# The second norm's factor moved behind the MLP's first product, the bias moved into gelu, one more bits buffer, four last transfers

## The chip, the core and the metric

The kernel runs on one core of a Trainium2 chip. The metric is the device time of one execution in microseconds (us). A core has five engines that run side by side: TensorE (PE in the profile; its weight loads are PEld), VectorE (DVE), ScalarE (ACT), GpSimd (POOL) and the sync engine (SP), which mostly issues DMA transfers. Three runs of the kernel before took 777.36 to 779.22 us, with a median of 778.76 us.

## What is computed

The input x has 2048 tokens of 512 values. It is normalised once (xn), and two branches read xn: attention with 32 heads of 16 values, and an MLP of width 1792 that normalises xn a second time. The result is x + attention(xn) + MLP(xn).

```python
xn = _layernorm(x)
q, k, v = split(xn @ wqkv)                 # 32 heads, Dh = 16
p = softmax(einsum("bhqd,bhkd->bhqk", q, k) * Dh ** -0.5)
attn = einsum("bhqk,bhkd->bqhd", p, v).reshape(B, S, D) @ wo
y = _layernorm(xn)
h = gelu(einsum("bsd,df->bsf", y, w1) + b1)  # tanh form, F = 1792
out = x + attn + einsum("bsf,fd->bsd", h, w2) + b2
```

As xn already has mean zero, the second norm is a product of each token's row with one number, 1 + r2[token].

## The kernel before, in words

Queries are cut into four tiles of 512 (qt) and heads into eight groups of four; a pair of these is a set g, 32 in all. For a set, keys come in 16 tiles of 128 (k). One unit is the score of one head against one key tile for 512 queries, a 128x512 block in PSUM (line 1037); there are 2048 units. Each unit takes one of two ways to its exponential. On the first, ScalarE reads two or three units at once (128x1024 or 128x1536) and writes exp to p_sb (line 1236). On the second, VectorE does it by bits for the four heads of a key tile together: four evictions write shifted 16-bit integers (128x512, line 1333, into ib, which lies in x_sb and in the tile it), and three more instructions of 128x2048 add constants to them (line 1354, TERMS = 4), so that the four bit patterns read as fp16 sum up to an approximation of exp. TensorE multiplies both kinds with the values va (line 1055) and sums them in one PSUM bank per set. NI is the number of bits buffers (five here; four of them are the space of x_sb), KD lists the seven key tiles of a set that may go by bits, and next_d decides when one is started; a key tile that is not started in time falls to ScalarE.

The MLP is done for each qt: build_mlp builds a 128x512 broadcast r2b of r2 (four products rt of r2 with ones on VectorE, line 1495, then TensorE, then a copy, line 1505), scales xnT into yT with two instructions of 128x2048 (lines 1507 and 1512), multiplies by w1 in 14 chunks (line 596 issues these), and adds b1 when VectorE evicts a chunk to ht (line 1528). After two query tiles, gelu runs in place over ht on ScalarE in one burst: four instructions of 128x3584 (line 1542) between two loads of activation tables. There are two such bursts. The product with w2 follows.

The order of all engines' instructions is set while the program is built, by a planner (_Plan): each piece has a cost, a due time (prio) and dependencies, and the planner places the piece that can start first on its engine, by due time among those that can start at nearly the same moment. KEEP favours a piece of the same TensorE mode as the one before. The planner's cost of a gelu burst is what tells it how long ScalarE is away; while it is, TensorE is given units for the bits way and matmuls with zeros (fill, line 1685) to do.

At the end, the last query tile's output is evicted by ScalarE and VectorE in turn into yT, and SP sends it in two transfers of 256 KB (build_final). At the start, the first norm's factor is made on GpSimd from the variance: an addition (line 743) and a power (line 745), for two token tiles at a time.

Of the kernel before, what the change touches and what calls it, by code (L numbers as in the profile page):

```python
# [1740 lines left out]
```

## Time and profile before

| what | value |
|---|---|
| median of three runs | 778.76 us (777.36 to 779.22) |
| profiled execution, its own time | 780.46 us |
| its span, first to last instruction | 778.7 us |
| mean granted TensorE clock | 0.991 of 2.4 GHz |
| ScalarE busy | 754.8 us, 97% |
| TensorE busy | 741.3 us, 95% |
| VectorE busy | 690.5 us, 89% |
| GpSimd busy | 49.4 us, 6% |

The profile is of one execution. Its own time is 1.7 us above the median of the runs, and its span is 1.8 us shorter than its own time. TensorE's busy time counts pipelined matmuls whose ends are modelled, and matmuls with zeros that fill gaps, so that its share is not a share of useful work. Busy time of ScalarE is the union of its instructions, which overlap at their ends.

### The profile page before, as it was taken

To read this page: it belongs to the slowest core of one execution; us is meant where nothing else is said; L and a number is where in the kernel's file an instruction comes from. 1 tells how busy PE (TensorE), PEld (TensorE's weight loads), DVE (VectorE), ACT (ScalarE), POOL (GpSimd) and SP (SyncE) were. 2 spreads that over 40 slices of the span, in tenths; PEclk is the share of its full clock that TensorE was granted. 3 is DMA by queue.
4 is the path that set the end of the run, shared out by engine and by line. 5 is a ranking of instruction groups with operands and counts; after the bars stand their busy time and mean duration, and the time that the engine had idled before them with its cause. 6 is when DMAs were issued, how large, how long until landed. Compare 5 with 4: busy or idle time off the path is not lost.

```text
span 778.7 us, 21921 instructions
## 1 busy us (share of the span) xinstructions
PE 741.3 (95%) x9344; PEld 242.0 (31%) x9344; DVE 690.5 (89%) x1196; ACT 754.8 (97%) x663; POOL 49.4 (6%) x81
## 2 busy tenths in 40 slices
PE   8999999999999999999899999999999989999996
PEld 3333223333323323333223333333233323333332
DVE  7857899999999988689999897989999999869795
ACT  5999899999999999999999999999999999999995
POOL 2300000020010000100001001100001000000001
PEclk9999899999999999999999999999999999999998
DMA  6300011234001300311010312320012101212001
GB/s 189 111 2 10 22 44 33 50 93 106 18 3 29 79 19 12 73 51 50 16 29 21 87 30 68 80 57 16 3 34 58 45 3 50 53 37 68 10 13 44
DMA packets 59157, 35.31 MB, mean 45 GB/s; under 512 B 41844, under 2 KB 50868, under 8 KB 59056
## 3 DMA queue, kind: packets, MB, share of 16 engines
q1 hardware_dynamic: 52576, 24.05, 11.3%
q0 software_dynamic: 4608, 8.39, 4.6%
q8 instruction: 74, 1.21, 0.7%
q10 hardware_dynamic: 1872, 1.44, 0.6%
q14 instruction: 27, 0.22, 0.1%
HBM read 26.08 MB, written 2.61 MB: 37 GB/s over the span
## 4 chain that ended last, share of the span: by engine, by line
ACT 37%; PE 32%; DVE 16%; issue 14%; DMA 0%; ACTq 0%; SPq 0%
ACT p_sb L1236 35%; PE ps L596 10%; PE ps L1037 10%; PE ps L1055 10%; DVE x_sb L1333 6%; DVE it L1354 4%; ACT ht L1542 1%; DVE it L1333 1%; DVE stats L731 1%; PE ps L1685 1%; DVE yT L1507 0%; DVE va L944 0%; DVE osb L1389 0%; DVE qc L918 0%; DMA x_sb<-in_A_x_dram 0%
## 5 line engine op out<-in xcount | busy, mean ns | idle before, releaser
L1236 ACT ACTIVATE p_sb<-ps 128x1024 bf16<-128x1024 f32 (+1 forms) x640 | 718.7, 1277 | 7.5 <-PE ps L1037 5.7
L1037 PE MATMUL ps<-qz,kt 32*128 32x512 bf16 x2048 | 317.1, 383 | 25.7 <-ACT p_sb L1236 13.8
L1333 DVE TENSOR_SCALAR x_sb<-ps 128x512 int16<-128x512 f32 x384 | 253.6, 681 | 21.7 <-PE ps L1037 20.6
L1354 DVE TENSOR_SCALAR it<-x_sb 128x2048 int16<-128x2048 int16 x288 | 191.0, 682 | 3.8 <-PE ps L1055 2.8
L1037 PEld LDWEIGHTS <-kt 32*128 32x128 bf16 x2048 | 86.6, 91 | 283.9 <-issue 278.4
L1055 PE MATMUL ps<-p_sb,va 128*32 128x512 bf16 x1568 | 154.1, 390 | 1.6 <-DVE x_sb L1333 0.7
L1055 PE MATMUL ps<-it,va 128*32 128x512 f16 x1536 | 124.7, 383 | 0.4 <-DVE it L1354 0.2
L1055 PEld LDWEIGHTS <-va 128*32 128x32 bf16 x3488 | 76.1, 95 | 133.0 <-issue 109.5
L1191 PE MATMUL ps<-ones_bf,zeros_bf 32*128 32x512 bf16 x187 | 70.0, 387 | 0.0
L1333 DVE TENSOR_SCALAR it<-ps 128x512 int16<-128x512 f32 x96 | 64.1, 681 | 3.7 <-PE ps L1037 3.2
L596 PE MATMUL ps<-w_sb,ht 128*32 128x512 bf16 x896 | 59.5, 381 | 0.1
L596 PE MATMUL ps<-yT,w_r 128*32 128x512 bf16 x896 | 58.5, 381 | 0.4
L1528 DVE TENSOR_SCALAR ht<-ps,b_sb 128x512 bf16<-128x512 f32 x56 | 41.5, 742 | 9.3 <-PE ps L596 9.2
L1354 DVE TENSOR_SCALAR it<-it 128x2048 int16<-128x2048 int16 x72 | 47.8, 684 | 0.2
L1685 PE MATMUL ps<-ones_bf,zeros_bf 128*32 128x512 bf16 x500 | 43.5, 388 | 0.0
L1055 PE MATMUL ps<-x_sb,va 128*32 128x512 f16 x384 | 38.4, 391 | 0.0
L1552 POOL DMA_DIRECT2D wkv<-in_A_x_dram x16 | 10.6, 666 | 419.7 <-DVE ot L1565 273.7
L596 PEld LDWEIGHTS <-w_r 128*32 128x32 bf16 x896 | 21.2, 96 | 23.7 <-issue 9.7
L596 PEld LDWEIGHTS <-ht 128*32 128x32 bf16 x896 | 20.7, 96 | 22.5 <-issue 8.3
L1389 DVE COPY osb<-ps 128x512 f32<-128x512 f32 x31 | 21.2, 685 | 5.0 <-PE ps L1055 4.6
L1542 ACT ACTIVATE ht<-ht 128x3584 bf16<-128x3584 bf16 x8 | 24.9, 3178 | 0.0
L1191 PEld LDWEIGHTS <-zeros_bf 32*128 32x128 bf16 x187 | 16.8, 91 | 13.1 <-issue 12.7
(98 smaller groups left out, 317.9 us busy)
## 6 DMA issues: line engine op xcount, KB each, us to landing
rlb<-rdram SPq DMA_DIRECT2D x31, 256.0 KB
w_r<-in_B_w_dram SPq DMA_DIRECT2D x56, 128.0 KB
wkv<-in_A_x_dram POOLq DMA_DIRECT2D x16, 256.0 KB, 2.9
wkv<-in_B_b_dram POOLq DMA_DIRECT2D x16, 256.0 KB, 4.3
w_sb<-in_B_w_dram SPq DMA_DIRECT2D x1, 1792.0 KB
out_dram<-ot SPq DMA_DIRECT2D x12, 128.0 KB
x_sb<-in_A_x_dram SPq DMA_DIRECT2D x2, 512.0 KB
ont<-ons SPq DMA_DIRECT2D x60, 16.0 KB
```

Of the source, the lines that this page charges most:

```text
L596: I(nc.tensor.matmul(dst[32 * j:32 * j + 32], lhsT=lhsT[:, 32 * j:32 * j + 32], rhs=rhs, start=start, stop=stop, tile_position=(0, 32 * j)))
L1037: I(nc.tensor.matmul(ps[:, bank, :], lhsT=kt[lo:lo + 32, s // 2, k * P:(k + 1) * P], rhs=qz[lo:lo + 32, (qt * NB + s // 2) % NQB, s % 2, : ...
L1055: I(nc.tensor.matmul(ps[32 * j:32 * j + 32, o_bank[g], :], lhsT=vals[:, h * VS:h * VS + 32], rhs=wts(j), start=pv_done[g] == 1, stop=end, ...
L1191: I(nc.tensor.matmul(ps[:, o_bank[g], :], lhsT=zeros_bf[32 * j:32 * j + 32, :], rhs=ones_bf[32 * j:32 * j + 32, :], start=False, stop=Fals ...
L1236: I(nc.scalar.activation(p_sb[:, s0:s1, :].rearrange("p a b -> p (a b)"), ps[:, b0:b0 + n, :].rearrange("p a b -> p (a b)"), AF.Exp, scale ...
L1333: I(nc.vector.tensor_scalar(out=ib[sl][:, j, :], in0=ps[:, pool.bank(key), :], scalar1=LEVEL, scalar2=0.0, op0=ALU.add, op1=ALU.max))
L1354: I(nc.vector.tensor_scalar(out=tb[x].rearrange("p j q -> p (j q)"), in0=ib[sl].rearrange("p j q -> p (j q)"), scalar1=float(SHIFT[t]), sc ...
L1389: e0 = add("DVE", dve(QW), lambda: I(nc.vector.tensor_copy(osb[:, i2, :], ps[:, o_bank[g], :])), pvs + before, pr - 1000, rel=(o_done(g),))
L1528: I(nc.vector.tensor_scalar(out=hq[:, fc, :], in0=ps[:, misc.bank(key), :], scalar1=b1_sb[:, fc:fc + 1], scalar2=None, op0=ALU.add))
L1542: I(nc.scalar.activation(out=hv, in_=hv, func=AF.Gelu_apprx_tanh, scale=1.0))
L1552: xb_ = add("POOL", 1.0, lambda: I(nc.gpsimd.dma_start(out=acc[:, c, :], in_=x2[qi * P:(qi + 1) * P, :])), wait, pr - 30, lat=XL)
L1685: I(nc.tensor.matmul(ps[32 * j:32 * j + 32, bank, :], lhsT=zeros_bf[:, 0:32], rhs=ones_bf[:], start=new, stop=new, tile_position=(0, 32 * ...
```

## The change

- The scaling of xnT into yT goes; the MLP's first product reads xnT itself. r2b becomes 1 + r2 in fp32, and VectorE multiplies with it as it evicts a chunk to ht. The products rt are made on GpSimd.
- b1 goes into gelu as its bias, an operand of one number per partition; each bias belongs to one chunk, so a burst is now 28 instructions of 128x512. Its cost for the planner is 28 times the cost of 512 columns.
- NI goes from 5 to 6. yT goes; the normalised rows of x and the last outputs use part of ht.
- The first norm's addition for the first four token tiles moves from GpSimd to VectorE.
- The last output leaves in four transfers of 128 KB, the third of them on ScalarE's queue.
- The planner's priorities get a nudge per piece, from a number per set (MIX), on some sets; MIX also shifts the threshold RES of next_d, which goes from 32 to 40. KEEP and some ten more constants change.

```diff
-    KEEP = 4.0
+    KEEP = 8.0
...
-                            key=lambda c: (c[1].prio - (self.KEEP if c[1].mode == same else 0.0),
+                            key=lambda c: (c[1].prio + self.nudge(c[1].seq)
+                                           - (self.KEEP if c[1].mode == same else 0.0),
...
-    NPU, NI, NTB, NON, NW1 = 15, 5, 4, 7, 4
+    NPU, NI, NTB, NON, NW1 = 15, 6, 4, 7, 4
...
-    yT = const.tile([P, JC, QW], BF, name="yT")
-    xn_r = yT
-    r2b = const.tile([P, QW], BF, name="r2b")
+    r2b = const.tile([P, QW], F32, name="r2b")
+    xn_r = yo = ht[:, 0, 4:8, :]
...
+    MIX = (0, 0, 0, 0, 0, 0, 636, 624, 0, 0, 0, 0, 0, 0, 0, 0, 0, 0, 37, 0, 0, 376, ...
-    OPEN, RES, RESL, SLK, ALP = 2, 32, 36, 45.0, 0.0
+    OPEN, RES, RESL, SLK, ALP = 2, 40, 36, 45.0, 0.0
-    RATE, QO, PO, AO, DO = 21.25, 45.0, 38.0, 40.0, 14.5
+    RATE, QO, PO, AO, DO = 21.25, 50.0, 38.0, 30.0, 14.5
...
+            def fes(sl=sl):
+                I((nc.gpsimd if g else nc.vector).tensor_scalar(
+                    out=wv1[:, sl], in0=mv[:, sl, 1], scalar1=LN_EPS, scalar2=None, op0=ALU.add))
...
-                I(nc.vector.tensor_scalar(out=rt[:, i, :], in0=ones_bf[:, 0:P],
+                I((nc.gpsimd if GM else nc.vector).tensor_scalar(out=rt[:, i, :], in0=ones_bf[:, 0:P],
...
-        e = add("DVE", dve(QW), lambda: I(nc.vector.tensor_copy(r2b[:], ps[:, misc.bank(rkey), :])),
-        y = add("DVE", dve(4 * QW, 0.52), lambda: I(nc.vector.tensor_tensor(
-            out=yT[:], in0=xnT[:, qt, :, :],
-            in1=r2b[:].unsqueeze(1).to_broadcast([P, JC, QW]), op=ALU.mult)),
-        y = add("DVE", dve(4 * QW, 0.52), lambda: I(nc.vector.tensor_tensor(
-            out=yT[:], in0=yT[:], in1=xnT[:, qt, :, :], op=ALU.add)), (y,), lo - 4)
+        y = add("DVE", dve(QW), lambda: I(nc.vector.tensor_scalar(
+            out=r2b[:], in0=ps[:, misc.bank(rkey), :], scalar1=1.0, scalar2=None, op0=ALU.add)),
...
-                I(nc.vector.tensor_scalar(out=hq[:, fc, :], in0=ps[:, misc.bank(key), :],
-                                          scalar1=b1_sb[:, fc:fc + 1], scalar2=None, op0=ALU.add))
+                I(nc.vector.tensor_tensor(out=hq[:, fc, :], in0=ps[:, misc.bank(key), :], in1=r2b[:],
+                                          op=ALU.mult))
...
-                for h0 in (0, half):
-                    hv = ht[:, i, h0:h0 + half, :].rearrange("p a b -> p (a b)")
-                    I(nc.scalar.activation(out=hv, in_=hv, func=AF.Gelu_apprx_tanh, scale=1.0))
-        gelu[0] = add("ACT", act(2 * FC * QW) + 2.9, fg, h_ops + hs, hi + 4)
+                for fc in range(FC):
+                    I(nc.scalar.activation(out=ht[:, i, fc, :], in_=ht[:, i, fc, :],
+                                           func=AF.Gelu_apprx_tanh, bias=b1_sb[:, fc:fc + 1], scale=1.0))
+        gelu[0] = add("ACT", dur + 2.9, fg, h_ops + hs + [cv_b1], hi + 4)
...
-        for c in (0, 2):
-            dma("SP", o2[q0 + c * P:q0 + (c + 2) * P, :].rearrange("(c p) d -> p c d", p=P),
-                yT[:, c:c + 2, :], outs[c:c + 2], ts_(NG) + c)
+        for c in range(TQ):
+            dma("QA" if c == 2 else "SP", o2[q0 + c * P:q0 + (c + 1) * P, :], yo[:, c, :],
+                (outs[c],), ts_(NG) + c)
```

The order changes nearly everywhere. Counted over the whole program, ScalarE has 284 exponentials of 128x1536 and 346 of 128x1024 where it had 289, 350 and one of 128x512; VectorE has 504 bit evictions of 128x512 and 378 bit terms of 128x2048 where it had 480 and 360; TensorE has 1544 matmuls of p_sb and 2016 of bit patterns with va where it had 1568 and 1920, and 496 matmuls with zeros of line 1685 (now 1693) where it had 500.

ScalarE at the first gelu burst, before (p_sb are the exponentials, ht the MLP's hidden layer):

```order
L1236 ACTIVATE p_sb<-ps 128x1536
L1542 ACT_TABLE_LOAD
L1542 ACTIVATE ht<-ht 128x3584 x4
L1236 ACT_TABLE_LOAD
L1236 ACTIVATE p_sb<-ps 128x1024
```

The same place in the changed order:

```order
L1248 ACTIVATE p_sb<-ps 128x1536
L1549 ACT_TABLE_LOAD
L1549 ACTIVATE ht<-ht,b_sb 128x512 x28
L1248 ACT_TABLE_LOAD
L1248 ACTIVATE p_sb<-ps 128x1024
```

Four instructions became 28, each with b_sb as a second operand; the burst comes after 221 instead of 247 exponentials.

VectorE where the first query tile's factor is made, before (x_sb and it are bits, rt and r2b the factor, osb a set's sum, kt keys):

```order
L1495 TENSOR_SCALAR rt<-ones_bf,r_83 128x128 x4
L1333 TENSOR_SCALAR x_sb<-ps 128x512
L1389 COPY osb<-ps 128x512
L1333 TENSOR_SCALAR x_sb<-ps 128x512
L1505 CAST r2b<-ps 128x512
L1333 TENSOR_SCALAR x_sb<-ps 128x512 x2
L1507 TENSOR_TENSOR yT<-xnT,r2b 128x2048
L1333 TENSOR_SCALAR x_sb<-ps 128x512
L1389 COPY osb<-ps 128x512
```

The same place in the changed order:

```order
L1401 COPY osb<-ps 128x512
L1345 TENSOR_SCALAR x_sb<-ps 128x512
L1366 TENSOR_SCALAR it<-it 128x2048
L1345 TENSOR_SCALAR x_sb<-ps 128x512 x2
L1366 TENSOR_SCALAR it<-x_sb 128x2048
L1519 TENSOR_SCALAR r2b<-ps 128x512
L1345 TENSOR_SCALAR x_sb<-ps 128x512
L1408 RECIPROCAL rc<-lc 128x16
```

The four rt and the 128x2048 product are gone from VectorE there, and the terms of a key tile's bits stand between its evictions. The rt now stand on GpSimd behind the second norm's factor:

```order
L798 TENSOR_SCALAR r_83<-r_83 128x16
L1508 TENSOR_SCALAR rt<-ones_bf,r_83 128x128 x4
L721 CAST ident_f<-ident_bf 128x128
L1508 TENSOR_SCALAR rt<-ones_bf,r_83 128x128 x4
L1560 DMA wkv<-in_A_x_dram 128x512 x4
```

The second four wait for TensorE to have read the first, and the loads of x into wkv, which the output sums start from, are queued behind them.

## Rows read from the trace of the kernel before

**Rows 1.** Page, part 1: busy us (share of the span) xinstructions

```profile
PE 741.3 (95%) x9344; PEld 242.0 (31%) x9344; DVE 690.5 (89%) x1196; ACT 754.8 (97%) x663; POOL 49.4 (6%) x81
```

**Rows 2.** Page, part 5: instructions by line | busy us, mean ns | idle

```profile
L1236 ACT ACTIVATE p_sb<-ps 128x1024 bf16<-128x1024 f32 (+1 forms) x640 | 718.7, 1277 | 7.5 <-PE ps L1037 5.7
```

**Rows 3.** Waits of ScalarE, whole span: us, times, longest us

```profile
ACT p_sb L1236 <- PE ps L1037: 5.7, 15, 1.3
```

**Rows 4.** Windows view, first to last exponential: busy us of each engine

```profile
12.25:768.86 756.61, 727.86 (x9245) 235.98 (x9242) 677.69 (x1161) 749.51 (x654) 43.45 (x60) 0.99 0.16 42
```

**Rows 5.** Lines by form, ScalarE, same columns

```profile
L1236 ACT ACTIVATE p_sb<-ps 128x1536 bf16<-128x1536 f32 x289 | 438.1, 1516 | 3.1 <-PE ps L1037 2.4
L1236 ACT ACTIVATE p_sb<-ps 128x1024 bf16<-128x1024 f32 x350 | 374.3, 1081 | 4.4 <-PE ps L1037 3.3
L1542 ACT ACTIVATE ht<-ht 128x3584 bf16<-128x3584 bf16 x8 | 24.9, 3178 | 0.0
L878 ACT ACTIVATE qz<-ps,maskq 128x256 bf16<-128x256 f32 x1 | 0.5, 474 | 0.6 <-PE ps L601 0.6
L865 ACT CAST kt<-ps 128x384 bf16<-128x384 f32 x1 | 0.5, 478 | 0.2 <-PE ps L601 0.2
L863 ACT CAST kt<-ps 128x128 bf16<-128x128 f32 x1 | 0.3, 265 | 0.1
```

**Rows 6.** Timeline of ScalarE at the first gelu burst: start us, us, what

```profile
288.29 1.28 ACT L1542 ACT_TABLE_LOAD   x1
289.58 12.43 ACT L1542 ACTIVATE ht<-ht 128x3584 bf16<-128x3584 bf16 x4
302.03 1.28 ACT L1236 ACT_TABLE_LOAD   x1
```

**Rows 7.** Lines by form, VectorE, GpSimd and TensorE: same columns

```profile
L1507 DVE TENSOR_TENSOR yT<-xnT,r2b 128x2048 bf16<-128x2048 bf16 x4 | 4.9, 1214 | 0.0
L1512 DVE TENSOR_TENSOR yT<-yT,xnT 128x2048 bf16<-128x2048 bf16 x4 | 4.9, 1215 | 0.0
L1495 DVE TENSOR_SCALAR rt<-ones_bf,r 128x128 bf16<-128x128 bf16 x16 | 2.9, 246 | 0.0
L1528 DVE TENSOR_SCALAR ht<-ps,b_sb 128x512 bf16<-128x512 f32 x56 | 41.5, 742 | 9.3 <-PE ps L596 9.2
L1565 DVE TENSOR_TENSOR ot<-ps,wkv 128x512 bf16<-128x512 f32 x12 | 8.2, 687 | 9.7 <-PE ps L596 9.7
L1333 DVE TENSOR_SCALAR x_sb<-ps 128x512 int16<-128x512 f32 x384 | 253.6, 681 | 21.7 <-PE ps L1037 20.6
L1354 DVE TENSOR_SCALAR it<-x_sb 128x2048 int16<-128x2048 int16 x288 | 191.0, 682 | 3.8 <-PE ps L1055 2.8
L1055 PE MATMUL ps<-it,va 128*32 128x512 f16 x1536 | 124.7, 383 | 0.4 <-DVE it L1354 0.2
```

**Rows 8.** Timeline of ScalarE, 68 to 90 us, with [idle before <-releaser]

```profile
74.47 7.00 ACT L1236 ACTIVATE p_sb<-ps 128x1536 bf16<-128x1536 f32 x6 [0.46 <-PE ps L1037]
82.00 1.45 ACT L1236 ACTIVATE p_sb<-ps 128x1536 bf16<-128x1536 f32 x1 [0.53 <-PE ps L1037]
84.75 1.02 ACT L1236 ACTIVATE p_sb<-ps 128x1024 bf16<-128x1024 f32 x1 [1.30 <-PE ps L1037]
86.34 4.63 ACT L1236 ACTIVATE p_sb<-ps 128x1536 bf16<-128x1536 f32 x4 [0.56 <-PE ps L1037]
```

**Rows 9.** Windows view: busy us per engine, granted clock, DMA share, GB/s

```profile
78.00:80.00 2.00, 2.00 (x17) 0.50 (x13) 1.85 (x5) 2.00 (x3) 0.00 (x0) 0.59 0.32 67
```

**Rows 10.** Timeline of VectorE and TensorE in that stretch

```profile
73.80 1.22 DVE L1507 TENSOR_TENSOR yT<-xnT,r2b 128x2048 bf16<-128x2048 bf16 x1
75.67 0.97 PE L1037 MATMUL ps<-qz,kt 32*128 32x512 bf16 x5 [0.45 <-DVE x_sb L1333]
```

**Rows 11.** Timeline of GpSimd at the start

```profile
7.12 0.29 POOL L743 TENSOR_SCALAR wv<-mv 128x2 f32<-128x2 f32 x1 [0.55 <-DVE mv L732]
```

**Rows 12.** Timeline of the sync engine's queue at the end

```profile
773.10 1.29 SPq L674 DMA_DIRECT2D out_dram<-yT  x2
```

More of the change, by code (lines that the diff above doesn't have):

```diff
@@ L215 @@
     nq = 0
+    nudge = staticmethod(lambda seq: 0.0)
     ready = None
@@ L740, in layernorm @@
             sl = slice(a, a + (4 if g else 2))
+            def fes(sl=sl):
+                I((nc.gpsimd if g else nc.vector).tensor_scalar(
+                    out=wv1[:, sl], in0=mv[:, sl, 1], scalar1=LN_EPS, scalar2=None, op0=ALU.add))
             def frs(sl=sl):
-                I(nc.gpsimd.tensor_scalar(out=wv1[:, sl], in0=mv[:, sl, 1], scalar1=LN_EPS,
-                                          scalar2=None, op0=ALU.add))
                 I(nc.gpsimd.tensor_tensor(out=r1[:, sl], in0=wv1[:, sl], in1=mhalf[:, sl],
                                           op=ALU.pow))
-            r = add("POOL", 1.4, frs, [st_op[t] for t in range(sl.start, sl.stop)] + [mk_half], pr)
+            r = add("POOL" if g else "DVE", 0.4 if g else 0.12, fes, [st_op[t] for t in range(sl.start, sl.stop)],
+                    pr - (0 if g else 20))
+            r = add("POOL", 1.0 if g else 0.75, frs, [r, mk_half], pr)
             for t in range(sl.start, sl.stop):
@@ L1077, in overdue, with nudge @@
                    for o in I.ready["PE"])
+    def nudge(seq):
+        m = MIX[stream["g"]]
+        return seq * (2 * m + 1) * 40503 % 65536 / 65536 * NUDGE if m else 0.0
     def next_d():
@@ L1095, in next_d @@
                 return
-            if g == stream["g"] and units_left(g) + HS * len(left_d[g]) < (RES if g < NG - 1 else RESL):
+            if g == stream["g"] and units_left(g) + HS * len(left_d[g]) < (
+                    RES + MIX[g] % 7 * 3 - 9 * (MIX[g] > 0) if g < NG - 1 else RESL):
                 continue
@@ L1504, in build_mlp @@
         d = add("PE", 0.25, ft, (c,), lo - 7, acq=((one, rkey), (misc, rkey)), dense=1.0)
-        e = add("DVE", dve(QW), lambda: I(nc.vector.tensor_copy(r2b[:], ps[:, misc.bank(rkey), :])),
-                (d,), lo - 506, rel=(one, misc.giver(rkey)))
-        y = add("DVE", dve(4 * QW, 0.52), lambda: I(nc.vector.tensor_tensor(
-            out=yT[:], in0=xnT[:, qt, :, :],
-            in1=r2b[:].unsqueeze(1).to_broadcast([P, JC, QW]), op=ALU.mult)),
-            [e] + y_use + [xt_op[t] for t in range(4 * qt, 4 * qt + 4)] + list(xn_op.values()),
-            lo - 5)
-        y = add("DVE", dve(4 * QW, 0.52), lambda: I(nc.vector.tensor_tensor(
-            out=yT[:], in0=yT[:], in1=xnT[:, qt, :, :], op=ALU.add)), (y,), lo - 4)
-        hs, ms = [], []
+        rt_use[0] = d
+        y = add("DVE", dve(QW), lambda: I(nc.vector.tensor_scalar(
+            out=r2b[:], in0=ps[:, misc.bank(rkey), :], scalar1=1.0, scalar2=None, op0=ALU.add)),
+                [d] + r2_use, lo - 506, rel=(one, misc.giver(rkey)))
+        hs = []
         for fc in range(FC):
@@ L1520, in build_mlp @@
                     list(w1_use.get(n - NW1, ())) + [st_op[NT - 1]], pr - 12, nb=pr - 18)
[L1522 to L1523 removed]
+            m = chain(key, pr, [(w1_r[:, n % NW1, jc, :], xnT[:, qt, jc, :]) for jc in range(JC)],
+                      [y, w] + [xt_op[t] for t in range(4 * qt, 4 * qt + 4)] + list(xn_op.values())
+                      + h_use[qt % 2], nb=pr - 4)[1]
             w1_use[n] = (m,)
[L1525 removed]
             def fe(fc=fc, key=key):
[L1528 to L1531 removed]
+                I(nc.vector.tensor_tensor(out=hq[:, fc, :], in0=ps[:, misc.bank(key), :], in1=r2b[:],
+                                          op=ALU.mult))
+            hs.append(add("DVE", dve(QW), fe, (m, y), pr - 500, rel=(one, misc.giver(key))))
+        r2_use[:] = hs
         if qt % 2 == 0:
@@ L1702 @@
     tc.mark_branch_hint_location("general", "LikelyTaken", [ET.Activation, ET.DVE, ET.PE, ET.SP])
-    I.fill = fill
+    I.fill, I.nudge = fill, nudge
     I.run()
```

48 lines of the change are left out of this document (23 added, 25 removed).

## Prediction, made before the change was run

> **What bounds the kernel.** I read the page first, for the engine that is full. ScalarE is busy 754.8 us, 97% of the span, TensorE 741.3 and VectorE 690.5 [rows 1]. Then the windows view, for where the rest of ScalarE's time lies: its first exponential starts at 12.25 us and the last ends at 768.86, and in these 756.61 us it is busy 749.51, VectorE only 677.69 [rows 4]. So 7.1 us of idle time stand between ScalarE and its own sum, and 5.7 of them are waits for TensorE's scores, in 15 places [rows 3]. The span is therefore about 12 us of start, ScalarE's sum, 7 us of waits and 10 us of end. The exponentials take 718.7 us of the sum [rows 2], gelu 24.9 [rows 5], four table loads 5. A step counts if it changes what ScalarE must do, what it waits for, or the two ends. VectorE's savings count only through the units that it takes over.
>
> **Exponentials moved to VectorE.** Before, 289 instructions of 1536 columns, 350 of 1024 [rows 5] and one of 512 make 802,816 columns in 718.7 us [rows 2], 0.895 ns a column with the fixed part in it. The changed order has 284 and 346: 790,528 columns, 12,288 fewer, which is 24 units of 512. At 0.895 ns that is 11.0 us less. This number is firm, since both kernels mix the two widths alike.
>
> **Gelu in 28 pieces instead of four.** A burst is one table load, 12.43 us of gelu and another load [rows 6]; with 3.18 us for the last piece, one piece follows the other by (12.43 - 3.18) / 3 = 3.08 us. A column costs 0.832 ns, from two copies on the same engine, (478 - 265) / 256 [rows 5], so 3584 columns are 2.98 us and 0.10 is fixed. A piece of 512 columns then takes at least 0.43 + 0.10 = 0.53 us, and 56 of them 29.5, 4.6 us more than the 24.9 of before. That is the lower bound. The bias is new: it is read per partition, which gelu before did not do. The nearest row is the one instruction with such an operand, qz with maskq: 474 ns for 256 columns, where the two copies give 372 between 128 and 384 columns [rows 5], so 0.10 us more. Whether this is hidden behind the piece before, the trace doesn't show, since qz stands alone. If it isn't, a piece takes 0.63 us, 56 take 35.2, and ScalarE gets 10.3 us more. That is the upper bound, and the value I take, because the row shows the price and nothing shows an overlap. So 4.6 to 10.3, taken 10.3: nearly all of the 11.0 is paid back.
>
> The Trainium skill speaks against this edit in the same place: its page ScalarE: Activation LUTs (What ACT_TABLE_LOAD costs) gives 280 ns and 0.833 ns a column for an ACTIVATE with a per-partition bias, 186 ns without, and an overlap of 93 ns between neighbours. By that a piece would take 0.614 us as an estimate, 56 of them 34.4, so 9.5 us more, and the forecast would be 775.3. The trace agrees on the piece without a bias; for the step of one with it, no run here shows it.
>
> **The burst against its plan.** The planner books a burst as 28 x 0.482 + 2.9 = 16.4 us; before it booked 14.9, and the trace has 1.28 + 12.43 + 1.28 = 15.0 [rows 6]. With 0.63 us a piece the burst takes 28 x 0.63 + 2.6 = 20.2, so TensorE comes to the end of what is laid beside the burst some 3.8 us early, twice, and stands until ScalarE frees a bank. That alone costs nothing, as ScalarE is then the late one. But an idle TensorE can come back at the lower of its two clocks. I put in one wait of the longest kind seen, 1.3 us [rows 3, 8], for the two bursts together; between 0 and the price of a full dip at both, 5.7 (next part).
>
> **The waits at 74 to 87 us.** Half of ScalarE's waiting is here: 0.46, 0.53, 1.30 and 0.56 us, 2.85 together [rows 8]. The granted clock is 0.59 in the slice 78 to 80 us [rows 9], that is, most of it at 1.2 instead of 2.4 GHz, and just before TensorE waited 0.45 us for an eviction that stood behind the 1.22 us of line 1507 on VectorE [rows 10]. The change takes this instruction, its pair and the four rt (246 ns each, rows 7) off VectorE here. I take it that the low clock goes and 2.85 us with it; bounds 0 and 2.85, and the same loss can come back elsewhere. What is late next here are bit terms: in the changed order they stand between the same evictions.
>
> **VectorE.** Off go 4 x (1.214 + 1.215) = 9.7 us, the rt 2.9 (union), and 56 evictions that fall from 742 ns to about the 687 of a product from PSUM with fp32, 3.1 us [rows 7]. On come 24 bit evictions at 681 ns and 18 terms at 682, 28.6 us. VectorE rises by about 13 us to 691 of the same stretch [rows 4], 91%. It is covered by its idle 79 us, as long as the pieces arrive spread; if not, they show as waits of TensorE for VectorE and then of ScalarE. TensorE gets 72 more matmuls of the value product net, at 124.7 / 1536 = 0.081 us [rows 7] at most 5.8 us, beside four fewer with zeros; it is full by the page only because zeros fill it. The sixth bits buffer, the nudges and the constants have no price of their own: they are in the count of units and in the waits. The rt on GpSimd are hidden by an engine that is idle 94% of the time [rows 1]; the loads queued behind them are due well ahead of the sums that use them. Each piece of gelu waits for VectorE, but the evictions are done before the burst is laid. I cost all these at 0, between -1 and +3.
>
> **Start and end.** GpSimd's addition of 0.29 us [rows 11] leaves the path to the first score and a shorter one on VectorE enters: -0.2, between -0.3 and 0. At the end the two transfers hold SP's queue for 1.29 us [rows 12]; with four, the last is half as large and still goes out when VectorE has its last eviction, behind one on the other queue: -0.2, between -0.6 and +0.2.
>
> **The sum.** -11.0 + 10.3 + 1.3 - 2.85 - 0.2 - 0.2 = -2.65 us. From the profiled execution's own 780.46 that gives 777.8; this execution lies 1.70 above the median of the runs, so on the footing of 778.76 it is 776.1.
>
> **Rivals.**
> - The bias is read while the piece before still runs. Then gelu costs 4.6, a burst 17.4 us against 16.4 booked, and no stall follows: -11.0 + 4.6 - 2.85 - 0.4 = -9.65, 769.1. For it: exponentials overlap heavily (438.1 + 374.3 us of durations in 718.7 of busy time, rows 2 and 5). Against: they have no such operand.
> - The low clock near 80 us stays or moves: -11.0 + 10.3 + 1.3 - 0.4 = +0.2, 779.0. For it: VectorE is given more bits there. Against: its longest instructions leave.
> - Slower: after each burst TensorE comes back at the low clock with ScalarE's two scored tiles as its only lead, and each time loses the 2.85 us that the dip near 80 us cost, while that dip stays: -11.0 + 10.3 + 5.7 - 0.4 = +4.6, 783.4. It decides from a stall of about 4 us, thus only with the full price of the bias. Against: TensorE has work laid for most of the burst.
> - The units leave ScalarE, but VectorE can't take them in time: TensorE's waits for x_sb evictions grow. This has the price of the second rival at most twice over, and I count it there.
>
> **How the numbers follow.** Forecast 0.42, hidden bias 0.25, clock stays 0.21, slower 0.12. What a measurement of this kernel can tell from no change is 0.3%, 2.3 us, so faster is below 776.4. The forecast's own range is 774.0 to 778.2, and 0.25 of its 0.42 lie below the bound; with 0.25 of the hidden bias and 0.02 of the clock that is 0.52. The same: 0.17 + 0.18 = 0.35. Slower: 0.12 and 0.01. The range of 8 in 10 reaches over the hidden bias and the clock case, and leaves out the slower one: 768.5 to 780.5.
>
> **What will show it.** Right: 630 exponentials with about 708 us busy; gelu with 0.63 us a piece and 35 us; no waits of ScalarE between 70 and 90 us; VectorE near 704 us. Wrong: gelu at 0.53 a piece; a granted clock below 1 behind a burst, with waits of ScalarE there of more than 2 us; ScalarE's waits above 10 us in all, spread over stretches where VectorE is full.

## The result, and the profile after

The changed kernel takes 784.83 us (median of 7 runs, 783.9 to 788.7) against 779.22 for the kernel before on the same chip (seven runs, the first three of which made the median of 778.76): ratio 1.0076, interval 1.0049 to 1.0103. The prediction of 776.1 was wrong in sign. The profiled execution of the changed kernel has a span of 785.0 us and took 786.79 itself, 2.0 above its median, so single terms below can be a little large. The seven runs differ in how much low clock they met (mean granted clock 0.992 at 783.9 to 784.4 us, 0.988 in the profiled one, 0.986 at 788.7), so a single stretch of low clock in the trace need not stand in the median execution.

The page, parts 1 and 5 of the kernel after (rows 1 and 2 of before answer to them):

```profile
PE 743.1 (95%) x9413; PEld 243.5 (31%) x9414; DVE 700.0 (89%) x1216; ACT 755.2 (96%) x701; POOL 61.6 (8%) x95
...
L1248 ACT ACTIVATE p_sb<-ps 128x1536 bf16<-128x1536 f32 (+1 forms) x630 | 709.5, 1270 | 12.9 <-PE ps L1043 11.1
```

The exponentials fell from 718.7 to 709.5 us, as the count of columns said. But ScalarE's sum is what it was, 755.2 for 754.8 [rows 1], and its idle time before an exponential went from 7.5 to 12.9 us [rows 2]. ScalarE's instructions by form, then VectorE's eviction:

```profile
L1248 ACT ACTIVATE p_sb<-ps 128x1536 bf16<-128x1536 f32 x284 | 428.4, 1509 | 7.1 <-PE ps L1043 6.2
L1248 ACT ACTIVATE p_sb<-ps 128x1024 bf16<-128x1024 f32 x346 | 367.8, 1075 | 5.8 <-PE ps L1043 4.8
L1549 ACT ACTIVATE ht<-ht,b_sb 128x512 bf16<-128x512 bf16 x56 | 34.5, 707 | 0.0
...
L1536 DVE TENSOR_TENSOR ht<-ps,r2b 128x512 bf16<-128x512 f32 x56 | 38.2, 682 | 2.5 <-PE ps L597 2.4
```

Gelu takes 34.5 us for 24.9 [rows 5]. ScalarE's waits (us, times, longest) against 5.7, 15, 1.3 [rows 3]:

```profile
ACT p_sb L1248 <- PE ps L1043: 11.1, 26, 1.6
...
ACT ht L1643 <- PE ps L597: 3.8, 2, 3.6
```

Where the new waits stand is read from ScalarE's timeline at the two bursts (start us, us, what, [idle before <-releaser]; rows 6 is the first of before):

```profile
256.81 1.28 ACT L1549 ACT_TABLE_LOAD   x1
258.10 17.26 ACT L1549 ACTIVATE ht<-ht,b_sb 128x512 bf16<-128x512 bf16 x28
275.38 1.28 ACT L1248 ACT_TABLE_LOAD   x1
276.67 4.62 ACT L1248 ACTIVATE p_sb<-ps 128x1024 bf16<-128x1024 f32 x4
282.17 1.02 ACT L1248 ACTIVATE p_sb<-ps 128x1024 bf16<-128x1024 f32 x1 [0.87 <-PE ps L1043]
284.48 3.87 ACT L1248 ACTIVATE p_sb<-ps 128x1536 bf16<-128x1536 f32 x3 [1.29 <-PE ps L1043]
...
601.69 17.25 ACT L1549 ACTIVATE ht<-ht,b_sb 128x512 bf16<-128x512 bf16 x28
...
625.04 1.02 ACT L1248 ACTIVATE p_sb<-ps 128x1024 bf16<-128x1024 f32 x1 [1.08 <-PE ps L1043]
626.64 2.37 ACT L1248 ACTIVATE p_sb<-ps 128x1536 bf16<-128x1536 f32 x2 [0.57 <-PE ps L1043]
```

TensorE's timeline in the same place, then the windows (us, busy us of PE, PEld, DVE, ACT, POOL, granted clock, DMA share, GB/s):

```profile
273.71 1.05 PE L597 MATMUL ps<-w_sb,ht 128*32 128x512 bf16 x16
277.75 0.61 PE L1043 MATMUL ps<-qz,kt 32*128 32x512 bf16 x3 [2.99 <-ACT p_sb L1248]
...
621.75 0.40 PE L1043 MATMUL ps<-qz,kt 32*128 32x512 bf16 x3 [3.77 <-ACT p_sb L1248]
```

```profile
276.00:278.00 2.00, 0.25 (x3) 0.10 (x2) 0.00 (x0) 1.99 (x3) 0.00 (x0) 0.84 0.00 0
278.00:280.00 2.00, 1.82 (x14) 0.46 (x15) 1.57 (x3) 2.00 (x3) 0.00 (x0) 0.50 0.00 0
...
362.00:366.00 4.00, 3.70 (x25) 0.72 (x22) 2.60 (x5) 3.62 (x4) 0.00 (x0) 0.59 0.00 0
...
618.00:620.00 2.00, 0.00 (x0) 0.00 (x0) 1.26 (x4) 1.98 (x3) 0.00 (x0) 1.00 0.00 0
...
622.00:624.00 2.00, 2.00 (x23) 0.61 (x20) 0.00 (x0) 1.96 (x2) 0.00 (x0) 0.52 0.00 0
...
78.00:80.00 2.00, 2.00 (x32) 0.60 (x21) 2.00 (x4) 2.00 (x3) 1.83 (x3) 1.00 0.04 4
```

TensorE stands 2.99 us for an exponential that itself stands behind the burst, comes back at 0.50 of its full clock (1.2 GHz), and ScalarE, which was the late one a moment ago, then waits for TensorE twice. The same is seen from 618 us, where TensorE stands 3.77 us. At 362 us there is one more stretch at the low clock, away from any burst and without such a stand (TensorE's longest wait in the 7 us before it is 0.30 us); the one at 78 to 80 us of before [rows 9] is gone (1.00).

The runs below are compared by one sum, worked out from ScalarE's records. When nothing waits, an exponential of 1024 columns ends 0.917 us behind the one before it and one of 1536 ends 1.343 us behind (the medians). Count times step is the exponentials' own need; what the steps exceed that by is called **lost**. The last column is the part of it that starts within 50 us of the end of the table load behind each burst.

The ratios are to runs of the kernel before on the same chip in the same round; their medians were 779.06 to 780.92 us. A ratio's interval reaches 0.2 to 0.3% to either side, so differences of 2 us between medians of two rounds say little. The last four columns are read from one profiled execution each.

| kernel | median us | ratio to before, 95% | exponentials | gelu | lost | of it behind bursts |
|---|---|---|---|---|---|---|
| before | 779.22 | | 709.6 | 24.9 | 15.5 | 2.4 |
| after | 784.83 | 1.0049-1.0103 | 698.7 | 34.5 | 22.8 | 7.1 |
| e10, no bias, long gelu | 773.19 | 0.9875-0.9921 | 698.7 | 24.9 | 19.5 | 5.2 |
| e1, no bias operand | 775.91 | 0.9924-0.9965 | 698.7 | 29.3 | 18.5 | 3.2 |
| e12, two sets a piece | 776.23 | 0.9937-0.9972 | 698.7 | 29.3 | 17.4 | 3.2 |
| e2, true length booked | 784.96 | 1.0037-1.0094 | 702.3 | 34.5 | 17.8 | 1.0 |
| e4, bias on VectorE | 779.38 | 0.9975-1.0011 | 702.3 | 24.9 | 22.3 | 1.0 |
| e8, no nudges | 790.94 | 1.0099-1.0149 | 704.1 | 34.5 | 19.2 | 7.5 |
| e3, before with bias in gelu | 793.25 | 1.0132-1.0199 | 709.6 | 34.5 | 18.2 | 5.7 |
| e5, before booked short | 796.26 | 1.0161-1.0214 | 713.2 | 24.9 | 28.1 | 10.9 |

From before to after that is -10.9 for exponentials, +9.6 for gelu, +7.3 lost, -0.3 at the start, +0.5 at the end: +6.2 of the spans' +6.3.

The traces of e5, e6, e7 and e8 have one exponential of 1024 columns more than their expectations below count (353, 349, 353 and 349), 0.9 us; the sums here go by the traces.

### The profile page after: what moved, and what is told of

Its sections match the earlier page's. It is cut to its first block, busy times and chain, and to the rows that moved or that the text cites. A ratio compares the mean times of both kernels' runs of the same rounds, so it can differ in the third digit from the quotient of the medians.

```text
span 785.0 us, 22159 instructions
## 1 busy us (share of the span) xinstructions
PE 743.1 (95%) x9413; PEld 243.5 (31%) x9414; DVE 700.0 (89%) x1216; ACT 755.2 (96%) x701; POOL 61.6 (8%) x95
## 3 DMA queue, kind: packets, MB, share of 16 engines
q10 hardware_dynamic: 2016, 1.57, 0.7%
## 4 chain that ended last, share of the span: by engine, by line
PE 41%; ACT 32%; DVE 13%; issue 12%; DMA 0%; POOL 0%; ACTq 0%; DVEq 0%; SPq 0%
ACT p_sb L1248 29%; PE ps L1043 14%; PE ps L1061 14%; PE ps L597 13%; DVE it L1366 4%; DVE x_sb L1345 3%; ACT ht L1549 3%; DVE it L1345 2%; DVE stats L735 1%; PE ps L1693 1%; DVE osb L1401 1%; DMA x_sb<-in_A_x_dram 0%; ACT L1248 0%; DVE va L950 0%; DVE ht L1536 0%
## 5 line engine op out<-in xcount | busy, mean ns | idle before, releaser
L1248 ACT ACTIVATE p_sb<-ps 128x1536 bf16<-128x1536 f32 (+1 forms) x630 | 709.5, 1270 | 12.9 <-PE ps L1043 11.1
L1345 DVE TENSOR_SCALAR x_sb<-ps 128x512 int16<-128x512 f32 x336 | 221.8, 680 | 18.4 <-PE ps L1043 17.1
L1366 DVE TENSOR_SCALAR it<-x_sb 128x2048 int16<-128x2048 int16 x252 | 168.0, 682 | 5.0 <-PE ps L1061 4.2
L1061 PE MATMUL ps<-it,va 128*32 128x512 f16 x1680 | 133.8, 383 | 0.3 <-DVE kt L906 0.2
L1345 DVE TENSOR_SCALAR it<-ps 128x512 int16<-128x512 f32 x168 | 111.7, 680 | 8.5 <-PE ps L1043 8.4
L1366 DVE TENSOR_SCALAR it<-it 128x2048 int16<-128x2048 int16 x126 | 83.7, 681 | 4.0 <-PE ps L1061 3.6
L597 PE MATMUL ps<-xnT,w_r 128*32 128x512 bf16 x896 | 58.4, 380 | 0.2 <-DVE ht L1536 0.2
L1536 DVE TENSOR_TENSOR ht<-ps,r2b 128x512 bf16<-128x512 f32 x56 | 38.2, 682 | 2.5 <-PE ps L597 2.4
L1549 ACT ACTIVATE ht<-ht,b_sb 128x512 bf16<-128x512 bf16 x56 | 34.5, 707 | 0.0
L1061 PE MATMUL ps<-x_sb,va 128*32 128x512 f16 x336 | 33.5, 388 | 0.2 <-DVE osb L1401 0.2
```

Of the source, the lines that this page charges most:

```text
L597: I(nc.tensor.matmul(dst[32 * j:32 * j + 32], lhsT=lhsT[:, 32 * j:32 * j + 32], rhs=rhs, start=start, stop=stop, tile_position=(0, 32 * j)))
L1061: I(nc.tensor.matmul(ps[32 * j:32 * j + 32, o_bank[g], :], lhsT=vals[:, h * VS:h * VS + 32], rhs=wts(j), start=pv_done[g] == 1, stop=end, ...
L1248: I(nc.scalar.activation(p_sb[:, s0:s1, :].rearrange("p a b -> p (a b)"), ps[:, b0:b0 + n, :].rearrange("p a b -> p (a b)"), AF.Exp, scale ...
L1345: I(nc.vector.tensor_scalar(out=ib[sl][:, j, :], in0=ps[:, pool.bank(key), :], scalar1=LEVEL, scalar2=0.0, op0=ALU.add, op1=ALU.max))
L1366: I(nc.vector.tensor_scalar(out=tb[x].rearrange("p j q -> p (j q)"), in0=ib[sl].rearrange("p j q -> p (j q)"), scalar1=float(SHIFT[t]), sc ...
L1536: I(nc.vector.tensor_tensor(out=hq[:, fc, :], in0=ps[:, misc.bank(key), :], in1=r2b[:], op=ALU.mult))
```

## The experiments

Two theories stood against each other. **A**: a piece of gelu with the bias takes longer than the planner books, so each burst ends behind the work laid for TensorE, TensorE stands, comes back at the low clock and ScalarE waits. **B**: the waits belong to the new, denser order itself.

### The length of the burst alone, order untouched

**e1_no_bias_operand** (b1 is not added):

```diff
-  func=AF.Gelu_apprx_tanh, bias=b1_sb[:, fc:fc + 1], scale=1.0))
+  func=AF.Gelu_apprx_tanh, scale=1.0))
```

> The changed kernel with its order untouched; only the bias operand of the 56 gelu pieces is left out (so b1 is not added). Theory A (a piece with a bias takes 0.613 us where the planner booked 0.482, so TensorE runs out of laid work 3 us before each burst ends, comes back at the lower clock and ScalarE waits): a piece falls to 0.52 us, 5.2 us directly; the burst lasts 17.2 us against 16.4 booked, TensorE's wait for ScalarE at its end falls from 3.0 us to under 1, the granted clock stays full behind both bursts, and some 8 us of ScalarE's waits there go too: 784.8 - 5.2 - 8 = about 771.5. Rival B (the waits behind the bursts come from the denser order, more bits on VectorE and out products bunched there, not from the stall): only the 5.2 us, about 779.5.

Measured: 775.91 us, between the two. A piece ends 0.520 us behind the one before it, against 0.613 with the operand, so the operand costs 0.093 us a piece even back to back and 5.2 us in all. The time fell by 8.9, that is 3.7 us more than the length, and the loss behind the bursts from 7.1 to 3.2 us. TensorE's longest stand is 0.62 us behind the first burst and 1.18 behind the second, and no low clock follows; two stretches stand elsewhere, from 376 and from 489 us.

```profile
L1549 ACT ACTIVATE ht<-ht 128x512 bf16<-128x512 bf16 x56 | 29.3, 614 | 0.0
```

**e10_no_bias_long_gelu** (as e1, in the four long instructions of before):

```diff
-  for fc in range(FC):
-      I(nc.scalar.activation(out=ht[:, i, fc, :], ..., bias=b1_sb[:, fc:fc + 1], scale=1.0))
+  for h0 in (0, FC // 2):
+      hv = ht[:, i, h0:h0 + FC // 2, :].rearrange("p a b -> p (a b)")
+      I(nc.scalar.activation(out=hv, in_=hv, func=AF.Gelu_apprx_tanh, scale=1.0))
```

> The kernel after, its order untouched, with gelu in 4 x 3,584 columns a burst; b1 is not added at all. It is the run e9_gpsimd_same_order without GpSimd's work. Theory A: 784.8 - 9.5 - 4.5 = 771 us, and no low clock behind a burst or at 362 us. Rival B: 775 us. Beside e1_no_bias_operand (775.9 us, gelu in 56 pieces of 0.52 us) it tells whether a burst that ends sooner than booked saves more than its own length: 4.2 us by its length alone, 771.7.

Measured: 773.19 us, between the two. With both loads of the table a burst lasts 15.0 us here, 17.2 in e1 and 19.8 in after, against 16.4 booked. From e10 to e1 the gelu grows by 4.4 us and the time by 2.7; from e1 to after it grows by 5.2 and the time by 8.9. A burst that ends sooner than booked seems to save less than its length: ScalarE then waits 0.97 us for TensorE behind two exponentials, and the loss behind the bursts is 5.2 us here for 3.2 in e1, though 2.7 against 4.4 us is hardly clear of the noise. One that ends later costs more than its length. No low clock stands behind either burst; one is seen at 533 us, which theory A didn't expect.

```profile
258.24 12.43 ACT L1550 ACTIVATE ht<-ht 128x3584 bf16<-128x3584 bf16 x4
...
271.99 2.37 ACT L1248 ACTIVATE p_sb<-ps 128x1024 bf16<-128x1024 f32 x2
275.33 7.14 ACT L1248 ACTIVATE p_sb<-ps 128x1024 bf16<-128x1024 f32 x6 [0.97 <-PE ps L1043]
```

**e12_gelu_two_sets_a_piece** (the bias operand kept):

```diff
-  for i in range(2):
-      for fc in range(FC):
-          I(nc.scalar.activation(out=ht[:, i, fc, :], in_=ht[:, i, fc, :],
+  for fc in range(FC):
+      I(nc.scalar.activation(out=ht[:, :, fc, :], in_=ht[:, :, fc, :],
```

> The kernel after, its order untouched, bias operand kept: one gelu instruction covers the same 128 rows of h in both query sets (128x2x512), 14 a burst instead of 28. By the steps measured, 0.613 us for 512 columns with the bias and 0.833 ns a column more (between 0.520 us for 512 and 3.080 us for 3,584 without it), one takes 1.04 us and a burst 14.6 us, as long as in e1_no_bias_operand and 2.6 us shorter than after. Theory A (the price behind the burst comes from its ending behind the work that is laid for TensorE): the time of e1_no_bias_operand, 776 us (775 to 777), faster than before, and no low clock behind a burst. Rival B (no more than the length counts): 784.8 - 5.2 = 779.6 us.

Measured: 776.23 us, ratio 0.9955 (0.9937 to 0.9972), as theory A said and as e1, which has another number of pieces and no operand but the same length. This version beats both kernels: 2.8 us below before and 8.6 below after, of which 5.2 are the two bursts' length. Rival B's 779.6 lies above all of its nine runs (774.8 to 778.4). The form's row, ScalarE's waits, its timeline and the windows behind the first burst:

```profile
L1548 ACT ACTIVATE ht<-ht,b_sb 128x1024 bf16<-128x1024 bf16 x28 | 29.3, 1134 | 0.0
```

```profile
ACT p_sb L1248 <- PE ps L1043: 6.0, 21, 1.1
```

```profile
257.97 14.66 ACT L1548 ACTIVATE ht<-ht,b_sb 128x1024 bf16<-128x1024 bf16 x14
272.64 1.28 ACT L1248 ACT_TABLE_LOAD   x1
273.94 6.97 ACT L1248 ACTIVATE p_sb<-ps 128x1024 bf16<-128x1024 f32 x6
```

```profile
272.00:274.00 2.00, 1.84 (x24) 0.70 (x25) 2.00 (x4) 1.97 (x3) 0.00 (x0) 1.00 0.00 0
274.00:276.00 2.00, 1.35 (x19) 0.49 (x12) 1.85 (x4) 2.00 (x2) 0.00 (x0) 1.00 0.00 0
276.00:278.00 2.00, 1.65 (x26) 0.55 (x28) 1.37 (x3) 2.00 (x3) 0.00 (x0) 1.00 0.00 0
```

TensorE has work to the end of the burst (1.84 and 1.35 of 2 us busy, where after has 0.25), the clock stays at 1.00 and six exponentials follow without a wait. Behind the second burst the clock is full too. One stretch of low clock is left, from 534 us, as in e10.

### The same from the side of the kernel before

**e3_before_bias_in_gelu**:

```diff
-  I(nc.vector.tensor_scalar(out=hq[:, fc, :], in0=ps[...], scalar1=b1_sb[:, fc:fc + 1], ..., op0=ALU.add))
+  I(nc.vector.tensor_copy(out=hq[:, fc, :], in_=ps[...]))
...
-  for h0 in (0, half):
-      I(nc.scalar.activation(out=hv, in_=hv, func=AF.Gelu_apprx_tanh, scale=1.0))
+  for fc in range(FC):
+      I(nc.scalar.activation(..., func=AF.Gelu_apprx_tanh, bias=b1_sb[:, fc:fc + 1], scale=1.0))
```

> The kernel before with its order untouched; only the bias moves from the eviction into 28 gelu pieces a burst, whose cost for the planner stays 14.9 us a burst where the pieces should take 19.8. Theory A: 9.6 us for the pieces, and TensorE stalls some 4.9 us at the end of each burst, comes back at the lower clock, and ScalarE waits 4 to 5 us behind each: 779.2 + 9.6 + 8 to 10 = 797 to 799. Rival B: the order of before has no such waits, so only the pieces: about 789.

Measured: 793.25 us, +13.5 on its before, between the two: 9.6 of gelu and, in the profile, 2.7 lost, 3.3 behind the bursts. At the end of the first burst TensorE is busy 0.94 of 4 us, then the clock falls, in an order that has none of the change in it:

```profile
304.00:308.00 4.00, 0.94 (x20) 0.34 (x12) 1.64 (x3) 3.97 (x6) 0.00 (x0) 1.00 0.00 0
308.00:313.00 5.00, 4.67 (x45) 1.24 (x44) 1.29 (x2) 3.99 (x4) 0.00 (x0) 0.66 0.01 3
```

**e5_before_burst_booked_short** (gelu as before, only its booked length 3.0 us less):

```diff
-  gelu_end[0] = I.now + act(2 * FC * QW) + 2.0
+  gelu_end[0] = I.now + act(2 * FC * QW) - 1.0
...
-  gelu[0] = add("ACT", act(2 * FC * QW) + 2.9, fg, h_ops + hs, hi + 4)
+  gelu[0] = add("ACT", act(2 * FC * QW) - 0.1, fg, h_ops + hs, hi + 4)
```

> The kernel before with one edit: the planner books each burst 3.0 us shorter than before (both lines that hold its length). No instruction's own work is changed; the plan gives ScalarE three more exps (352 of 1,024 columns and 290 of 1,536 instead of 350 and 289: 2 x 0.917 + 1.343 = +3.2 us). Theory A (TensorE runs out of work laid for it before the burst's true end and comes back at the low clock): after both bursts the first exps wait and the granted clock stands at half for some us, +2 to +4 us a burst, 779.7 + 3.2 + 6 = 789 us (786 to 791). Rival B (the after's waits come from its denser order and not from the booked length): nothing at the bursts, 783 us.

Measured: 796.26 us. The loss behind the bursts went from 2.4 to 10.9 us, more than theory A's 4 to 8. Behind the second one TensorE had stood (1.80 us busy of 5) and then ran at half its clock for 20 us:

```profile
626.00:631.00 5.00, 1.80 (x23) 0.51 (x19) 2.65 (x6) 4.97 (x4) 0.00 (x0) 1.00 0.02 8
631.00:642.00 11.00, 10.92 (x77) 1.95 (x77) 8.13 (x13) 8.85 (x9) 0.00 (x0) 0.52 0.00 0
642.00:652.00 10.00, 10.00 (x74) 1.84 (x66) 5.88 (x10) 7.19 (x6) 0.00 (x0) 0.50 0.01 2
```

But the loss elsewhere rose as well, by 4.1 us (28.1 - 10.9 against 15.5 - 2.4): laying the order anew has a price of its own, so not all of the 10.9 need come from the booked length.

### Other ways to place or book the bias

**e2_true_burst_cost**:

```diff
-  dur = 2 * FC * act(QW)
+  dur = 2 * FC * 0.613
```

> The changed kernel with one number changed: the planner books 0.613 us for a gelu piece instead of 0.482, 20.1 us a burst. The order is planned anew; ScalarE gets 286 and 347 exponentials, 8 units more, 3.7 us. Theory A: TensorE has work to the end of each burst, no low clock there, 8 us of waits go: about 780.5. Rival B: the waits stay, about 788.

Measured: 784.96 us, no gain, which theory A's number missed. Its mechanism did go: no low clock in the span before the last 2 us and 1.0 us lost behind the bursts for 7.1. ScalarE's waits are 6.6 us for 11.1:

```profile
ACT p_sb L1248 <- PE ps L1043: 6.6, 22, 1.1
```

But the plan with the longer burst leaves three more exponentials on ScalarE, 0.917 + 2 x 1.343 = 3.6 us, which eats most of the 5.0; the rest is in the 2.0 us by which the profiled execution of after lies above its median. Booking the truth repairs the stall, not the length.

**e4_bias_on_vector** (and gelu in four long instructions a burst, as in e10):

```diff
+  I(nc.vector.tensor_scalar(out=hq[:, fc, :], in0=hq[:, fc, :], scalar1=b1_sb[:, fc:fc + 1], ..., op0=ALU.add))
...
-  dur = 2 * FC * act(QW)
+  dur = act(2 * FC * QW)
```

> The changed kernel with the bias added by VectorE in a second instruction of 128x512 behind each eviction and gelu in four pieces of 128x3584 a burst, booked as in the kernel before. The order is planned anew with 286 and 347 exponentials, 8 units more than the changed kernel, 16 fewer than before. Theory A: gelu is back at 24.9 us and its plan fits, so 784.8 - 9.6 - 8 + 3.7 = about 771, faster than both. Rival B: the waits behind the bursts stay, 779; and if VectorE's 56 further instructions, some 11 us, make it late, more.

Measured: 779.38 us, the time of before and rival B's number, but not for its reason: only 1.0 us is lost behind the bursts, as theory A had it. The 56 additions cost VectorE 345 ns each, 19.3 us (the expectation had 11); ScalarE gets the same three exponentials back, and 22.3 us are lost, nearly all elsewhere. VectorE is busy 706.3 us, 91% of the span, where after has 700.0. That the fuller VectorE makes these waits fits, but isn't shown, since the order is laid anew too.

```profile
L1540 DVE TENSOR_SCALAR ht<-ht,b_sb 128x512 bf16<-128x512 bf16 x56 | 19.3, 345 | 0.7
```

**e6_bias_on_gpsimd** (as e4, with the addition on GpSimd, planned):

```diff
+  I(nc.gpsimd.tensor_scalar(out=hq[:, fc, :], in0=hq[:, fc, :], scalar1=b1_sb[:, fc:fc + 1], ..., op0=ALU.add))
+  hs.append(add("POOL", 2.0, fb, (e, cv_b1), pr - 400))
```

> The kernel after with the bias added by GpSimd in place on ht (56 instructions of 128x512, booked 2.0 us each) and gelu in 4 x 3,584 columns a burst again. The plan gives ScalarE 348 + 286 exps (4 more than after: +4.5 us). Theory A: gelu is 9.5 us shorter than after and bursts end as booked, so the stalls go too (-4 to -5): 784.8 - 9.5 + 4.5 - 4.5 = 775 us (773 to 778). Rival B: waits stay, 784.8 - 9.5 + 4.5 = 780 us. If GpSimd slows VectorE's instructions beside it, more than that.

Measured: 792.77 us, ratio 1.0156 (1.0131 to 1.0181), worse than both theories. A longer gelu is not in it (24.9 us): 31.1 us are lost, two waits of nearly 3 us among them. One is at 405 us, behind weights from DRAM that TensorE waited 2.24 us for. The other is behind the second burst, in and behind which TensorE is at half its clock from 590 to 604 us, with work all the time (12.85 of 13 us busy):

```profile
402.29 1.83 PE L597 MATMUL ps<-xnT,w_r 128*32 128x512 bf16 x16 [2.24 <-DMA w_r<-in_B_w_dram]
...
607.25 7.06 ACT L1248 ACTIVATE p_sb<-ps 128x1536 bf16<-128x1536 f32 x6 [2.79 <-PE ps L1043]
...
590.00:603.00 13.00, 12.85 (x76) 2.42 (x76) 11.29 (x20) 12.97 (x6) 2.96 (x6) 0.51 0.33 67
```

**e9_gpsimd_same_order** (as e6, but behind each eviction, outside the plan):

```diff
   I(nc.vector.tensor_tensor(out=hq[:, fc, :], in0=ps[...], in1=r2b[:], op=ALU.mult))
+  I(nc.gpsimd.tensor_scalar(out=hq[:, fc, :], in0=hq[:, fc, :], scalar1=b1_sb[:, fc:fc + 1], ..., op0=ALU.add))
```

> The kernel after, its order on TensorE, VectorE and ScalarE untouched (346 + 284 exps): the bias is added by GpSimd in place right behind each eviction, outside the plan, and gelu is 4 x 3,584 columns a burst again. Theory A (the bias operand on ScalarE, and TensorE short of work behind bursts that end late): gelu 9.5 us shorter, the stalls behind the bursts go (-4 to -5): 784.8 - 14 = 771 us, plus up to 6 us where GpSimd's 56 x 1.76 us slow VectorE's 2,048-column instructions beside them (682 to 717 ns in the run e6_bias_on_gpsimd): 771 to 777, taken 773. Rival B (the waits are in the order itself): 784.8 - 9.5 = 775 us without that, 775 to 781 with it.

Measured: 781.41 us, ratio 1.0016 (1.0000 to 1.0032). It is e10 plus GpSimd's 56 additions, which cost 8.2 us on a kernel whose GpSimd is otherwise busy 8% of the time. No low clock is in its span up to the last 3 us. VectorE's 2,048-column terms take 714 ns (682 in after), and 26.1 us are lost:

```profile
L1366 DVE TENSOR_SCALAR it<-x_sb 128x2048 int16<-128x2048 int16 x252 | 175.8, 714 | 5.0 <-PE ps L1061 4.2
```

```profile
L1538 POOL TENSOR_SCALAR ht<-ht,b_sb 128x512 bf16<-128x512 bf16 x56 | 104.4, 1904 | 263.2 <-DVE ht L1536 258.9 <-PE ps L1061 4.3
```

### The order

**e8_no_nudges**:

```diff
-  MIX = (0, 0, 0, 0, 0, 0, 636, 624, ..., 777, 751)
+  MIX = (0,) * 32
```

> The kernel after with the table of nudges all zero. The plan gives ScalarE 348 + 286 exps instead of 346 + 284 (+4.5 us). Theory A: gelu still ends 3 us behind its booked end twice, so the low clock stands behind both bursts and the waits stay: 784.8 + 4.5 = 789 us. Rival B (the nudges' order makes the waits): the waits go, 784.8 + 4.5 - 7 = 782 us.

Measured: 790.94 us. The low clock still stands behind both bursts (7.5 us lost there; the first in the row below), so the nudges don't make it. By the spans (789.2 and 785.0) they are worth 4.2 us in after, by leaving five exponentials fewer to ScalarE (-5.4) and an end 2.3 us shorter, at 3.6 us more lost. The medians lie 6.1 apart, but come from two rounds whose kernels before differ by 1.7.

```profile
275.00:277.00 2.00, 0.14 (x2) 0.10 (x1) 0.51 (x1) 1.99 (x3) 0.00 (x0) 0.62 0.03 8
```

**e7_before_factor_on_gpsimd**:

```diff
-  I(nc.vector.tensor_scalar(out=rt[:, i, :], ...
+  I(nc.gpsimd.tensor_scalar(out=rt[:, i, :], ...
...
-  c = add("DVE", 0.6, fm, ...
+  c = add("POOL", 1.7, fm, ...
```

> The kernel before with one edit: the four instructions that spread the second norm's factor (rt) are on GpSimd, as in the kernel after. The plan gives ScalarE 352 + 290 exps (+3.2 us). If these four on VectorE made the low clock near 78 us, it goes and -2.5 us with it: 779.7 + 3.2 - 2.5 = 780.4 us. If the two long VectorE instructions that scale yT made it, which this kernel keeps, it stays: 783 us.

Measured: 790.01 us, ratio 1.0112, far above both. The low clock near 78 us stays, so the rt alone didn't make it:

```profile
78.00:80.00 2.00, 2.00 (x15) 0.52 (x18) 1.92 (x5) 2.00 (x2) 0.00 (x0) 0.61 0.10 17
```

Three more such stretches came, at 263, 406 and 614 us (the first and the last at the bursts), and ScalarE's waits for TensorE rose to 14.2 us, from four small instructions that changed engine and the order laid anew with them. This profiled execution took 794.48 us, 4.5 above its median, so these rows are on the bad side.

**e11_before_keep_8**:

```diff
-  KEEP = 4.0
+  KEEP = 8.0
```

> The kernel before with one constant changed as in the kernel after: what the order gives to staying in TensorE's mode (KEEP) is 8.0 instead of 4.0. The plan then gives ScalarE 346 exps of 1,024 columns and 285 of 1,536 instead of 350 and 289, 9.0 us less by the steps measured (4 x 0.917 + 4 x 1.343). If the exps that the kernel after saves come from this constant and a newly laid order brings no waits of its own: 779.7 - 9.0 = 771 us. If an order that was not matched to the chip brings waits and low clocks as in e5_before_burst_booked_short and e7_before_factor_on_gpsimd (+10 us each): 781 us.

Measured: 797.62 us, ratio 1.0210 (1.0189 to 1.0231): 9.0 us of exponentials less, and 43 us lost for 15.5. ScalarE's waits:

```profile
ACT p_sb L1236 <- PE ps L1037: 24.1, 67, 1.8
```

This run also bears on the dip near 78 us of before. The rt and both long products still stand on VectorE there (line 1507 at 72.58 us, 1512 behind it), and yet the clock is full:

```profile
72.58 1.22 DVE L1507 TENSOR_TENSOR yT<-xnT,r2b 128x2048 bf16<-128x2048 bf16 x1
...
78.00:80.00 2.00, 1.75 (x21) 0.49 (x20) 2.00 (x5) 2.00 (x3) 0.00 (x0) 1.00 0.00 1
```

So the units that ScalarE gives away say little by themselves about an order. In e5, e7 and e11 small edits to the planner of before raised the loss by 10 to 28 us.

## Why the prediction was wrong, step by step

Two steps failed: the price of the burst against its plan, and the new order, which was put at 0. The forecast of -2.65 would have been +0.75 with the first alone put right and +2.45 with the second alone; measured is +5.6. One of the prediction's own signs of being wrong came: a granted clock below 1 behind a burst, with 2.16 us of ScalarE's waits there (0.87 and 1.29).

**Exponentials, -11.0:** right. 709.5 us busy against about 708; by steps -10.9.

**Gelu, +10.3:** right in kind, a little large: 0.613 us a piece instead of 0.63, +9.6. The value chosen at the upper bound was the one to choose; e1 shows that the operand's price isn't hidden (0.093 us of the 0.10 read from qz, whose operand is a scale). The Trainium skill, ScalarE: Activation LUTs (What ACT_TABLE_LOAD costs), gave 0.614 us a piece as an estimate from its figures; the trace agrees, with 0.613.

**The burst against its plan, +1.3: the first step that failed.** The working saw the 3.8 us for which TensorE would stand (2.99 and 3.77 measured), named the low clock, bounded the price at 5.7, and then took 1.3 "for the two bursts together". Measured behind the bursts: 7.1 us lost for 2.4, +4.7, and e12 takes 3.9 of these away by the burst's length alone. The mechanism was named and the +4.7 lies within its bounds; the value taken was too small by 3.4. The argument used against the third rival, that TensorE has work laid for most of the burst, was no argument: what decides is whether it lasts to the end. That rival (783.4, chance 0.12) had the mechanism behind the bursts right. That its sum comes within 1.5 us of 784.83 is in part luck: it kept the dip near 80 us, which went, and had nothing for the new order.

**Low clock at 74 to 87 us, -2.85:** right in size, -2.5 in the first 100 us, but not for the reason given. The prediction had it go because line 1507, its pair and the rt leave VectorE there. In e7 the rt are gone from VectorE and the low clock stays; in e11 all of them are still there and it is gone (1.00 from 78 to 80 us). So these instructions alone don't make it, the order around them decides, and what in the order does is open. That the term came out is partly luck.

**The new order, 0 between -1 and +3: the second step that failed.** Outside the bursts and the first 100 us the loss is 6.0 us before and 11.1 after, +5.1. Of the 11.1, 2.9 are lost at the low clock at 362 us, which no other run of this order has; e1, e10 and e12 have theirs at other places, so whether the burst's length moves it is open. In e12, with the length mended, 9.6 remain, +3.6. The prediction gave the sixth bits buffer, the nudges and the constants no price and took VectorE's idle time to cover its 13 us of new work. VectorE itself came out as said (700.0 us busy for about 704), so that sum was not the fault. What in the order makes the loss isn't settled: without the nudges 7.1 us remain there (e8), for more exponentials on ScalarE, and e4 loses more there with a fuller VectorE, both in orders laid anew.

**Start and end:** -0.3 for -0.2, and +0.5 for -0.2: the copy at line 1643 waits 3.6 us for TensorE's last products where before it waited 2.6. What the two extra transfers cost or save no run tells apart.

The three terms of waits make -1.55 together in the forecast (1.3 - 2.85 + 0) and +7.3 in the traces (4.7 - 2.5 + 5.1). With that, -10.9 + 9.6 + 7.3 is the slower kernel. Had gelu kept its length, the same order would have taken 773 us (e10, which leaves b1 out); with the pieces merged over the two sets the whole change takes 776 (e12). So the length of the bursts, with what it does to TensorE, decides between faster and slower here, and the rest of the order's loss stays unexplained.

## What to carry to other kernels

When an order is planned ahead, a mis-booked instruction costs more than its own length if the engine beside it runs dry: 5.2 us of unplanned bias became 8.6. Booking the true length alone gained nothing here (e2), as the plan then left more work to ScalarE; shortening the burst did (e12). So compare every booked duration with the trace first, and where a step's working finds a stall of some us on TensorE, price it with the low clock behind it, not with a typical wait. Pieces that share a per-partition operand can be one instruction over several buffers, which here took the fixed part off 28 of 56 pieces.
